# Chunked attention and a Fourier-mixed MLP: later stores of untouched weight blocks, and ten slab loads moved into the next product

## The chip, the cores and the metric

The kernel runs on one core of one Trainium2 chip. The metric is the device time of one execution in microseconds (us); less is better. All arithmetic is in single precision.

## The reference, cut to what matters

```
# B, H, S, D = 8, 8, 576, 64;  chunks of 64 tokens, 9 a sequence
scores = q_c @ k_c^T / sqrt(D)              # inside each chunk
x = softmax(scores) @ v_c                   # -> (B, S, 512)
u = x + real(fft(fft(x, axis=1), axis=2))
un = (u - mean(u)) / sqrt(var(u) + 1e-6)    # along the last axis
out = u + max(un @ w_ch1, 0) @ w_ch2        # w_ch1: 512 x 2048, w_ch2: 2048 x 512, given in double precision
```

## The kernel before, in words

**Groups.** The 4608 tokens are cut into nine groups of 512 (`NG = 9`). Each group passes through `mlp(g)`: a first product with `w_ch1` and a second one with `w_ch2`. Attention and Fourier mixing of batch b (`attention`, `fourier`, joined in `side(b)`) are emitted in slices between the steps of the product of the group before it. The whole instruction order is written out by hand (`manual_schedule`). The main loop counts steps: `t` goes up by one for every `yield` of `mlp`. Group 0 takes steps 1 to 16 for its first product and 17 to 32 for its second (`KF = 16` row blocks each); `begin[1]` is 32. `ready_at[0]` is 2 * 16 - 5 = 27.

**Each engine works its queue in order.** SP issues nearly all loads and stores (908 of the DMAs), so a load stands behind every store that the program names before it; all of them go into one hardware queue, q1, and are served by 16 DMA engines.

**Weights.** The weights come as 32 pieces of 512 KB of doubles. Pieces 0 to 15 make `w1` (the tile `wa`), pieces 16 to 31 make `w2` (the tile `wb`), one a row block: piece 16 + m is row block m of `w2`. `load_weight` (L348) issues a load. `round_weight` turns doubles into floats: a head for piece i (DVE L372, L382; ACT L364, L367, L370) and a tail for piece i - 1 (DVE L379, L380, L388), after which the raw space is free and the next load is issued. `round_next` does the next piece; the counter is `n_w`. The two spaces that hold the last pieces are rows of `xall` that `keep2` (POOL L1095) writes afterwards.

**Block forms of the products.** From group 1 on, both products are done in seven half-size products instead of eight. The weight blocks and their sums that these need are written to DRAM while group 0 runs, `s1` for the first product and `s2` for the second, and are read back as slabs:

- `keep2(i)` makes four sums of `w2` blocks on POOL; `keep2_store` (L1107) stores them to `s2`.
- `keep2_whole(i)`, for i = 0 to 3, stores three blocks that need no sum, straight from `w2`: row blocks 2i, 2i+1 and 8+2i, 8+2i+1. It is three DMAs of 256 KB (L1114).
- `keep1(pair)` makes the sums of `w1` (POOL L1078) in the space of `w2` rows that are done with; `keep1_store` (L1082) stores them to `s1`.

For `keep2_whole` the loop body has, behind the call of `round_next`:

```
while n_whole < HF // 2 and n_w > KF + HF + 2 * n_whole + 2:
    keep2_whole(n_whole)
    n_whole += 1
keep2_store()
```

`KF + HF` is 24, so the four calls come as soon as 26, 28, 30 and 32 pieces have been counted.

**Slabs.** `fetch(1)` (L1179) loads the next of 196 slabs of 256 KB for the first product (28 a group, groups 2 to 8) into a ring of `NS1 = 10` in `wa`. Ten are fetched ahead when group 1 is at its middle, and every turn of `up_halves` (28 a group, the matmuls of L1309) fetches one more into the slot that the turn has read. So the last ten turns of a group fetch the first ten slabs of the next one. `fetch(2)` (L1184) does the like for the second product of groups 1 to 6 (`down_halves`, L1363).

**The last two groups.** Groups 7 and 8 (`FEW = 7`) do their second product in `down_few`: 26 quarter-size products (L1427), listed in `PRODUCTS`. Their slabs, 512 KB each, come by `fetch(3)` (L1182) through a ring of ten, one after each product. Twenty-three of these blocks are sums that `make_rest` makes on POOL and DVE (L1156) from the middle of group 6 to the end of the first product of group 7; it reads its inputs (L1145) and stores the sums (L1163) on SP too.

Of the kernel before, what the change touches and what calls it, by code (L numbers as in the profile page):

```python
# [16 lines left out]
def kernel(  # L17
# [43 lines left out]
    KF = DFF // 128  # L61
# [41 lines left out]
    NO, HF = 7, KF // 2  # L103
# [3 lines left out]
    NS1, NS2, Z1, Z2 = 10, 3, 2 * 2 * 128, HF * HM  # L107
# [958 lines left out]
    def parts1(pair):  # L1066
        a11, a12, a21, a22 = w1_part(pair, 0, 0), w1_part(pair, 0, 2), w1_part(pair, 1, 0), w1_part(pair, 1, 2)
        o1, o2, o4 = (made1(pair, j) for j in range(3))
        return a11, o2, o1, a21, a12, o4, a22
# [46 lines left out]
    def block_of(name):  # L1116

        if name[0] == "s":
            return s3[STORED.index(name)]
        o, k = (2, "dw".index(name)) if name in "dw" else ({"b1": 0, "b2": 0, "b3": 4 + "12".index(name[2]), "b4": 4 + "12".index(name[2])}[name[:2]], (int(name[1]) - 1) % 2)  # L1120
        return s2[o, :, k * Z3:(k + 1) * Z3]
# [49 lines left out]
    FEW = NG - 2  # L1171
    first_of = {1: 1, 2: 1}
    n_slab = {1: 0, 2: 0, 3: 0}

    def fetch(which):
        i = n_slab[which]
        if which == 1 and i < HF // 2 * NO * (NG - 2):
            pair, o = divmod(i % (HF // 2 * NO), NO)
            nc.sync.dma_start(out=slab1[i % NS1].rearrange("p k r f -> p (k r f)"), in_=s1[pair, UP[o]])  # L1179
        elif which == 3 and i < NR2 * (NG - FEW):  # L1180
            to = slab3[i % NS3].rearrange("p m e -> p (m e)")
            nc.sync.dma_start(out=to, in_=block_of(PRODUCTS[i % NR2][1]))  # L1182
        elif which == 2 and i < NO * (FEW - first_of[2]):
            nc.sync.dma_start(out=slab2[i % NS2].rearrange("p m e -> p (m e)"), in_=s2[i % NO])  # L1184
        n_slab[which] = i + 1
# [3 lines left out]
    def operands(h1, m):  # L1189

        nc.vector.tensor_tensor(out=xs[:, m], in0=h1[:, m, hi], in1=h1[:, HF + m, hi], op=ALU.add)  # L1191
        nc.vector.tensor_tensor(out=ys[:, m], in0=xs[:, m], in1=h1[:, m, lo], op=ALU.subtract)
        nc.gpsimd.tensor_tensor(out=h1[:, m, hi], in0=h1[:, m, lo], in1=h1[:, m, hi], op=ALU.subtract)  # L1193
# [94 lines left out]
    def up_halves(g):  # L1288
        unT = unTs[g]
        h1 = one_p.tile([128, KF, G * 128], FP32, tag="big", name="h1")  # L1290
        t1, t2, t4 = tt_1 if g == 1 else (tt[:, o] for o in range(3))
        rhs = (unT[:, 0:2, lo], t2, t1, unT[:, 0:2, hi], unT[:, 2:4, lo], unT[:, 2:4, hi], t4)
        for pair in range(HF // 2):
            pas, pbs = {}, {}
            for turn_, o in enumerate(UP):
                if g == 1:
                    w = parts1(pair)[o].rearrange("p k (r f) -> p k r f", r=2)
                else:
                    w = slab1[((g - 2) * HF // 2 * NO + pair * NO + turn_) % NS1]
                for r in range(2):  # L1300
                    m = 2 * pair + r
                    a, b = (tmp_1 if g == 1 else tmp)[:, r, 0], (tmp_1 if g == 1 else tmp)[:, r, 1]
                    if o == 0:
                        pas[r] = ps_f.tile([128, 2, 256], FP32, tag="ff", name="pa")
                    if o == 1:
                        pbs[r] = ps_f.tile([128, 2, 256], FP32, tag="ff", name="pb")
                    dst = (pas, pbs, pas, pbs, pas, pas, pbs)[o][r][:, (0, 0, 1, 1, 0, 1, 1)[o]]
                    for kk in range(2):
                        nc.tensor.matmul(  # L1309
                            out=dst, lhsT=w[:, kk, r], rhs=rhs[o][:, kk],  # L1310
                            start=(o in (0, 1) and kk == 0), stop=(kk == 1), skip_group_check=True,
                        )
                    if o == 0:
                        nc.scalar.copy(a, dst)  # L1314
                        nc.vector.tensor_tensor(out=b, in0=pbs[r][:, 0], in1=a, op=ALU.add)  # L1315
                    elif o == 2:
                        nc.vector.tensor_tensor(out=a, in0=dst, in1=b, op=ALU.add)  # L1317
                        if g == 1 and pair == 0:
                            combined(1, r, True)
                    elif o == 3:  # L1320
                        nc.vector.tensor_tensor(out=h1[:, HF + m, hi], in0=dst, in1=a, op=ALU.add)
                        if pair > 0 and g < FEW:
                            operands(h1, m - 2)
                    elif o == 4:
                        nc.scalar.activation(out=h1[:, m, lo], in_=dst, func=ACTF.Relu)  # L1325
                    elif o == 5:
                        nc.vector.tensor_tensor(out=h1[:, m, hi], in0=dst, in1=b, op=ALU.add)
                        nc.scalar.activation(out=h1[:, m, hi], in_=h1[:, m, hi], func=ACTF.Relu)
                    elif o == 6:
                        nc.vector.tensor_tensor(out=h1[:, HF + m, lo], in0=dst, in1=b, op=ALU.add)  # L1330
                        nc.scalar.activation(out=h1[:, HF + m], in_=h1[:, HF + m], func=ACTF.Relu)  # L1331
                if g > 1:
                    fetch(1)
                if pair == HF // 4 and turn_ > 0 and g >= FEW:
                    sums(h1, EARLY.split()[turn_ - 1:turn_], nc.vector if g == FEW else nc.gpsimd)
                if turn_ in (1, 3, 5, 6):
                    yield h1
        for m in (HF - 2, HF - 1) if g < FEW else ():
            operands(h1, m)
# [67 lines left out]
    def down_few(g, h1):  # L1407
        banks, begun = {}, set()
        left = [sum(p[3].count(f"{i + 1}{j + 1}") for p in PRODUCTS for j in range(2)) for i in range(G)]
        sums(h1, ["a24=a23+a24"])  # L1410
        for o, (a, _, bank, reads, then) in enumerate(PRODUCTS):
            w, lhs = slab3[((g - FEW) * NR2 + o) % NS3], block_a(h1, a)
            half = int(bank.isupper())
            if bank not in banks:
                if half:
                    banks[bank] = banks[bank.lower()]
                else:
                    banks[bank] = ps_f.tile([128, 2, 256], FP32, tag="ff", name="dn")
                begun.add(bank)
                fresh = True  # L1420
            else:
                fresh = False
            dst, k = banks[bank][:, half], o // 2
            if o % 2 and g + 1 < NG and k in range(5, 5 + 2 * G, 2):
                turned(g + 1, (k - 5) // 2)
            for m in range(4):
                nc.tensor.matmul(  # L1427
                    out=dst, lhsT=lhs[:, m], rhs=w[:, m],
                    start=(fresh and not half and m == 0), stop=(m == 3), skip_group_check=True,
                )  # L1430
            for sign_, i, j in zip(reads[0::3], reads[1::3], reads[2::3]):
                i, j = int(i) - 1, int(j) - 1
                n = groups[g][i]
                to = os_[:, i, j * HM:(j + 1) * HM]
                base = to if (i, j) in begun else natural(n)[:, j * HM:(j + 1) * HM]
                begun.add((i, j))
                nc.vector.tensor_tensor(out=to, in0=base, in1=dst, op=ALU.add if sign_ == "+" else ALU.subtract)
                left[i] -= 1
                if left[i] == 0:
                    store(n, os_[:, i])  # L1440
            sums(h1, then.split())
            fetch(3)
            if o % 2 == 0:
                continue
            if g + 1 < NG:
                for j in range(G):
                    if k == 3 + 2 * j:
                        normed(g + 1, j)
                    if k == 5 + 2 * j and j >= 2:
                        combined(g + 1, j - 2)  # L1450
            yield
# [7 lines left out]
    with tc.manual_schedule():  # L1459
# [22 lines left out]
        n_w = 2  # L1482
# [40 lines left out]
        ready_at = [begin[g] + (2 * KF - 5 if g < first_of[2] else 2 * HF + 4) for g in range(NG)]  # L1523
# [12 lines left out]
        n_whole, n_kept, late, rest_ = 0, 0, [], None  # L1536
        conv2 = chain(conv2)
        t = 0
        for g in range(NG):
            for _ in mlp(g):  # L1540
# [24 lines left out]
                    if t <= 2 or t < KF and t % 4 == 0 or t >= KF + 3:  # L1565
                        round_next()

                while n_whole < HF // 2 and n_w > KF + HF + 2 * n_whole + 2:
                    keep2_whole(n_whole)
                    n_whole += 1  # L1570
                keep2_store()
# [22 lines left out]
                for _ in range(2 if t > begin[1] else 0):  # L1594
                    if put_off:
                        b, t0_, r, o = put_off.pop(0)
# [60 lines left out]
```

## Time and profile before

| | |
|---|---|
| runs | 1063.61, 1063.99, 1064.34 us; median 1063.99 us |
| the profiled execution | 1063.73 us, of which the profile's span is 1061.9 us |
| TensorE (PE) busy | 1043.3 us, 98% of the span |
| VectorE (DVE), GpSimd (POOL), ScalarE (ACT) busy | 626.5, 431.9, 315.5 us |
| DMA | 219.10 MB, 206 GB/s on the mean |
| mean granted TensorE clock | 0.998 |

From the span's start, in us: 0 to 50 the attention and the Fourier mixing of batch 0; about 50 to 116 the first product of group 0; 116 to 191 its second product, with batch 1 beside it and the rounding of `w2`; 191 to 249 the first product of group 1 and so on; from 868.0 to 916.8 the first product of group 7, to 964.3 its second, to 1012.8 the first product of group 8, and its second to the end.

A page of the profile gives for each engine the time in which it worked. Rows by window (a stretch of the span) give the same for that stretch, with the clock that TensorE was granted, the busy share of the 16 DMA engines, and what they moved. A timeline row begins with the start and the time taken, and ends, where the engine was idle before it, with the idle time and what ended it. L numbers are lines of the kernel before. A row of SP is the issue of a DMA, not its run.

### The profile page before, as it was taken

The numbers are of one execution on the slowest core, as the hardware profiler recorded it, in microseconds if no ns is written. First come the engines' busy times: TensorE is split into PE (matmuls) and PEld (weight loads), VectorE is DVE, ScalarE is ACT, GpSimd is POOL, SyncE is SP. The second block draws the span as 40 slices with busy tenths as digits, with TensorE's granted clock in tenths as the row PEclk, the third lists the DMA queues.
The fourth block names the chain that finished last, engine by engine and source line by source line (L and its number), as shares of the span: only waits on it lengthen the run. The fifth ranks groups of instructions, "written<-read, shape, count | busy, mean of one in ns | idle before, by whom it ended". The sixth has DMA issues, their size and how long they took to land.

```text
span 1061.9 us, 20222 instructions
## 1 busy us (share of the span) xinstructions
PE 1043.3 (98%) x7482; PEld 851.6 (80%) x7482; DVE 626.5 (59%) x1339; ACT 315.5 (30%) x744; POOL 431.9 (41%) x555
## 2 busy tenths in 40 slices
PE   7999999999999999999999999999999999999998
PEld 6645444788888888888888888888888888888887
DVE  4798986974567465664565645745664666443332
ACT  4688573233113311332022312331133103201200
POOL 3410119753425151244134421514252777660282
PEclk9999999999999999999999999999999999999999
DMA  8767675687688447973678357944753759998364
GB/s 169 221 197 213 163 218 199 203 233 230 231 215 230 134 142 214 250 207 108 186 229 223 118 169 231 250 131 155 215 168 102 269 187 353 363 399 279 89 216 142
DMA packets 167088, 219.10 MB, mean 206 GB/s; under 512 B 77228, under 2 KB 111020, under 8 KB 161614
## 3 DMA queue, kind: packets, MB, share of 16 engines
q1 hardware_dynamic: 155978, 211.98, 64.8%
q0 software_dynamic: 9024, 4.91, 2.1%
q8 instruction: 60, 0.98, 0.4%
q10 hardware_dynamic: 1988, 0.92, 0.3%
q14 instruction: 38, 0.31, 0.1%
HBM read 183.61 MB, written 34.08 MB: 205 GB/s over the span
## 4 chain that ended last, share of the span: by engine, by line
PE 79%; DVE 6%; DMA 4%; ACT 3%; POOL 3%; SPq 2%; issue 2%; DVEq 0%; ACTq 0%; POOLq 0%
PE pa L1309 20%; PE pb L1309 15%; PE pb L1363 14%; PE pa L1363 11%; PE dn L1427 7%; PE pt L399 2%; SPq L265 2%; PE mix L840 2%; PE xp L501 2%; PE z L722 1%; DMA xall<-in_moe_w_ch_dram 1%; PE up L1219 1%; PE sc L451 1%; POOL h L1207 1%; POOL part L1156 1%
## 5 line engine op out<-in xcount | busy, mean ns | idle before, releaser
L1309 PE MATMUL pa<-unT,wa 128*128 128x256 f32 x736 | 175.3, 381 | 0.2 <-DVE xall L1317 0.2
L1309 PEld LDWEIGHTS pa<-unT,wa 128*128 128x128 f32 x736 | 138.1, 190 | 19.6 <-DVE xall L1317 0.6
L1309 PE MATMUL pb<-wa 128*128 128x256 f32 x448 | 106.6, 381 | 0.0
L1309 PEld LDWEIGHTS pb<-wa 128*128 128x128 f32 x448 | 84.3, 190 | 11.5
L1363 PE MATMUL pa<-wb,h 128*128 128x256 f32 x384 | 87.2, 380 | 0.0
L1363 PE MATMUL pb<-wb,h 128*128 128x256 f32 x384 | 86.4, 379 | 0.0
L1193 POOL TENSOR_TENSOR h<-h 128x256 f32<-128x256 f32 x48 | 40.8, 858 | 98.2 <-DVE wb L1191 91.6
L1363 PEld LDWEIGHTS pa<-wb,h 128*128 128x128 f32 x384 | 71.8, 190 | 9.7
L1363 PEld LDWEIGHTS pb<-wb,h 128*128 128x128 f32 x384 | 72.0, 190 | 9.4
L1044 POOL DMA_DIRECT2D out_dram<-wb x28 | 18.8, 674 | 121.8 <-DVE wb L1380 71.9
L1315 DVE TENSOR_TENSOR wa<-pb,wa 128x256 f32<-128x256 f32 x56 | 23.7, 424 | 63.5 <-ACT wa L1314 63.5
L1309 PE MATMUL pb<-unT,wa 128*128 128x256 f32 x256 | 60.6, 379 | 0.1
L1325 ACT ACTIVATE h<-pa 128x256 f32<-128x256 f32 x64 | 24.6, 384 | 115.0 <-PE pa L1309 114.1
L1260 PE MATMUL dn<-wb,h 128*128 128x512 f32 x128 | 58.7, 608 | 0.0
L1314 ACT COPY wa<-pa 128x256 f32<-128x256 f32 x56 | 20.9, 372 | 121.4 <-PE pa L1309 121.4
L1309 PEld LDWEIGHTS pb<-unT,wa 128*128 128x128 f32 x256 | 48.6, 190 | 7.1 <-DVE wa L1315 0.5
L1207 POOL TENSOR_TENSOR h<-h 128x512 f32<-128x512 f32 x34 | 42.8, 1276 | 27.2 <-ACT h L1331 24.1
L1309 PE MATMUL pa<-wa 128*128 128x256 f32 x224 | 53.9, 383 | 0.0
L483 ACT COPY pT<-pt 128x512 f32<-128x512 f32 x36 | 21.0, 582 | 105.8 <-PE pt L399 105.5
L1331 ACT ACTIVATE h<-h 128x512 f32<-128x512 f32 x64 | 40.0, 630 | 39.5 <-DVE h L1330 39.1
L1219 PE MATMUL up<-unT,wa 128*128 128x512 f32 x108 | 49.4, 598 | 0.0
L857 POOL TENSOR_TENSOR xall<-y,xall 128x513 f32<-128x513 f32 x14 | 22.3, 1590 | 61.1 <-DVE y L851 45.0
(312 smaller groups left out, 2136.6 us busy)
## 6 DMA issues: line engine op xcount, KB each, us to landing
wa<-s SPq DMA_DIRECT2D x196, 256.0 KB
wb<-s SPq DMA_DIRECT2D x42, 1024.0 KB
wb<-s SPq DMA_DIRECT2D x32, 512.0 KB
xall<-in_moe_w_ch_dram SPq DMA_DIRECT2D x22, 512.0 KB
q<-in_q_dram SPq DMA_DIRECT2D x96, 112.0 KB
k<-in_k_dram SPq DMA_DIRECT2D x96, 112.0 KB
s<-part SPq DMA_DIRECT2D x32, 256.0 KB
v<-in_v_dram SPq DMA_DIRECT2D x124, 64.0 KB
```

The costliest lines, as they stand in the source:

```text
L265: eng.dma_start(out=t[p0:p0 + np_], in_=src[b, :, c * CH:c * CH + np_, :].rearrange("h p d -> p h d"))
L857: eng.tensor_tensor(out=x[:, 0:w], in0=y[:, 0:w], in1=x[:, 0:w], op=ALU.add)
L1193: nc.gpsimd.tensor_tensor(out=h1[:, m, hi], in0=h1[:, m, lo], in1=h1[:, m, hi], op=ALU.subtract)
L1207: eng.tensor_tensor(out=out_, in0=a, in1=b, op=op)
L1219: nc.tensor.matmul(out=up, lhsT=w1[:, kk, m * 128:(m + 1) * 128], rhs=unT[:, kk], start=(kk == 0), stop=(kk == KD - 1), skip_group_check=True,
L1260: nc.tensor.matmul(out=dn, lhsT=h1[:, m, s * 128:(s + 1) * 128], rhs=w2[:, m, :], start=(m == 0), stop=(m == KF - 1),)
L1309: nc.tensor.matmul(out=dst, lhsT=w[:, kk, r], rhs=rhs[o][:, kk], start=(o in (0, 1) and kk == 0), stop=(kk == 1), skip_group_check=True,)
L1315: nc.vector.tensor_tensor(out=b, in0=pbs[r][:, 0], in1=a, op=ALU.add)
L1325: nc.scalar.activation(out=h1[:, m, lo], in_=dst, func=ACTF.Relu)
L1331: nc.scalar.activation(out=h1[:, HF + m], in_=h1[:, HF + m], func=ACTF.Relu)
L1363: nc.tensor.matmul(out=dst, lhsT=lhs[:, m], rhs=w[:, m], start=(o in (0, 2) and m == 0), stop=(m == HF - 1), skip_group_check=True,)
L1427: nc.tensor.matmul(out=dst, lhsT=lhs[:, m], rhs=w[:, m], start=(fresh and not half and m == 0), stop=(m == 3), skip_group_check=True,)
```

## The change

Two things are moved; nothing is added or left out.

1. `keep2_whole(0)` to `keep2_whole(3)` are no longer tied to the count of rounded pieces. They come one a step at `t` = 24, 25, 26 and 27 (`t > ready_at[0] - 4`), ahead of that step's `keep2_store`.
2. The first ten slabs of the last group's first product are no longer fetched in the last ten turns of group 7's `up_halves`. When `n_slab[1]` has reached 28 * 6 = 168, group 7 stops fetching; the ten are fetched in group 7's `down_few` after its products 10 to 19, one each, behind that product's `fetch(3)`.

```diff
@@ up_halves @@
-                if g > 1:
+                if g > 1 and (g != FEW or n_slab[1] < HF // 2 * NO * (FEW - 1)):
                     fetch(1)
@@ down_few @@
             sums(h1, then.split())
             fetch(3)
+            if g == FEW and 10 <= o < 10 + NS1:
+                fetch(1)
             if o % 2 == 0:
                 continue
@@ main loop @@
-                while n_whole < HF // 2 and n_w > KF + HF + 2 * n_whole + 2:
+                if n_whole < HF // 2 and t > ready_at[0] - 4:
                     keep2_whole(n_whole)
                     n_whole += 1
                 keep2_store()
```

## The prediction

> **What bounds the kernel now.** I read the page's busy times first, then the windows, to see in which stretches the busiest engine has anything to lose, then what TensorE (PE) waits for, and then the queues that feed that wait.
>
> ```profile
> PE 1043.3 (98%) x7482; PEld 851.6 (80%) x7482; DVE 626.5 (59%) x1339; ACT 315.5 (30%) x744; POOL 431.9 (41%) x555
> ```
>
> PE is idle for 18.6 us of 1061.9. The windows (length, then busy time of PE, PEld, DVE, ACT and POOL, then the granted clock, DMA share and GB/s) say where:
>
> ```profile
> 0.00:50.00 50.00, 42.32 (x516) 31.16 (x516) 29.47 (x87) 26.56 (x67) 21.42 (x48) 1.00 0.79 201
> ...
> 150.00:200.00 50.00, 45.32 (x243) 25.97 (x241) 39.60 (x65) 19.34 (x52) 38.58 (x32) 0.97 0.64 203
> 200.00:300.00 100.00, 99.66 (x856) 85.45 (x857) 61.78 (x136) 26.76 (x69) 48.02 (x67) 1.00 0.70 221
> ...
> 916.00:965.00 49.00, 48.58 (x233) 42.24 (x232) 19.88 (x46) 2.34 (x5) 28.94 (x24) 1.00 1.02 394
> ```
>
> 7.7 us lie in the first 50, which the change does not touch, 4.7 us between 150 and 200, and 4.3 us behind the last products. From 200 to the end of PE's work only fractions are left. PE's waits after 200 (sum, times, longest) are three rows; the only one in the stretches of the second edit is the first:
>
> ```profile
> PE dn L1427 <- POOL h L1207: 0.4, 1, 0.4
> PE pb L1309 <- DVE h L1321: 0.3, 1, 0.3
> PE pa L1309 <- DVE xall L1317: 0.2, 1, 0.2
> ```
>
> So the change can win in two places: about 2.5 of the 4.7 us at 150 to 200, and at most 0.5 us near 930. It can lose wherever it makes PE wait.
>
> The big wait at 150, in PE's timeline, is the mixing matmul behind ACT's copy of zf:
>
> ```profile
> 155.25 0.49 PE L840 MATMUL mix<-ce,zf 128*128 128x129 f32 x2 [2.47 <-ACT zf L773]
> ```
>
> ACT had waited for DVE's zs (L752, L756). The DVE timeline shows why those were late (the bracket is the idle time before a row):
>
> ```profile
> 144.72 0.43 DVE L372 TENSOR_SCALAR power<-xall 128x512 uint32<-128x512 uint32 x1 [0.75 <-DMA xall<-in_moe_w_ch_dram]
> ...
> 146.62 0.67 DVE L388 TENSOR_TENSOR wb<-wb,power 128x512 f32<-128x512 f32 x1
> 149.83 0.43 DVE L372 TENSOR_SCALAR power<-xall 128x512 uint32<-128x512 uint32 x1 [2.54 <-DMA xall<-in_moe_w_ch_dram]
> ...
> 152.32 0.75 DVE L752 TENSOR_TENSOR zs<-more_z,zs 128x580 f32<-128x580 f32 x1
> ```
>
> DVE stood 2.54 us for a weight piece, with the zs operations queued behind it. SP's queue shows what was ahead of that piece:
>
> ```profile
> 134.38 0.35 SPq L348 DMA_DIRECT2D xall<-in_moe_w_ch_dram  x1
> ...
> 136.86 3.53 SPq L348 DMA_DIRECT2D xall<-in_moe_w_ch_dram  x2
> 140.44 1.53 SPq L1114 DMA_DIRECT2D s<-wb  x3
> 142.02 0.63 SPq L1082 DMA_DIRECT2D s<-wa  x1
> 143.06 3.66 SPq L348 DMA_DIRECT2D xall<-in_moe_w_ch_dram  x2
> ```
>
> The three L1114 are `keep2_whole(0)`: 768 KB in front of the load issued at 143.06.
>
> **Edit 1, the stores of whole blocks.** Emission moves from the steps in which the pieces are counted to steps 24 to 27. SP's L1082 at 142.02 belongs to step 20, so the first call leaves its place ahead of the load at 143.06 and lands behind the last load (146.4).
>
> Load, issue to the DVE that it released: 134.38 to 138.40 is 4.02 us; 136.86 to 141.41 is 4.55; the second of that pair, issued about 140.05 (the group's end, 140.39, less one issue of 0.35), to 144.72 is 4.67; the one in question, 143.06 to 149.83, is 6.77. Its issue doesn't move: it waits for DVE's L382 at 142.95. With one 256 KB store ahead of it, as the 4.55 one had, it lands at 147.6; the bounds are 147.1 and 147.7. DVE itself is free at 147.29. So DVE resumes at 147.3 to 147.7 and gains 2.1 to 2.5 us; I take 2.3. A load at 140.05 that is also quicker, with less behind it (4.02 instead of 4.67), would free DVE by up to 0.65 earlier and let the gain reach 2.7.
>
> Does the gain reach the end? Step by step. zs needs ACT's L747, done at 148.84, and would start at 152.32 - 2.3 = 150.0: no wait. The last piece, issued at 146.38, lands by 146.4 + 4.67 = 151.05; DVE wants it at 153.85 - 2.3 = 151.55: no wait, with 0.5 us to spare. PE finishes the matmuls before the gap at 152.78 and the mixing could start at 155.25 - 2.3 = 152.95. Behind it stand the last tails on DVE (159.16), POOL's `keep2` sums, which write the rows that those tails free (POOL L1095 at 155.55 and 159.85 both wait for DVE L380), then POOL L857 at 164.48, statistics, `un`, the transposes, L1031 to L1033, and the first L1309 of group 1 at 191.39. PE, ACT, DVE and POOL each run in order, no link of this chain is tied to a clock of its own, so it moves as a block. PE has no work to be late with: its idle 0.40, 0.53 and 1.14 us at 171 to 182 stay. From 191 on PE is nearly solid and hands the shift on to the end. Minus 2.3 us.
>
> What the moved stores cost where they go: twelve SP issues of about 0.45 us. The first two calls fit into 146.8 to 161.4, where SP had held nine of them anyway. Calls three and four come behind L1107 of step 25, at about 162 to 166, six issues, 2.7 us of SP, 1.5 MB. Behind them on SP are stores, L1107 of yall, gated by POOL until 169.4 anyway, and L1082; no load stands there before L252 at 184.45. Their readers come late: `fetch(2)` first at 229.7, and POOL's reuse of the space (the second keep2 set at 178.36 and 183.39). DMA moved 63 GB/s between 171.2 and 182.4, so the 3.6 us that 1.5 MB takes at 420 GB/s fits. Cost nothing, covered by that lull; without it, up to 3.6 us on the load of L252.
>
> **Edit 2, the ten slabs.** Out of 894 to 926 go ten issues and 2.6 MB. There DMA is full, but PE's only wait is the 0.42 us for POOL sums, which start when the matmuls allow and not when a DMA lands: gain 0, bound 0.4. In: ten issues behind ten `fetch(3)` in products 10 to 19, PE time 936.6 to about 953.
>
> ```profile
> 936.60:951.30 14.70, 14.70 (x74) 12.94 (x73) 6.49 (x13) 0.59 (x1) 8.85 (x7) 1.00 1.02 419
> 951.30:964.30 13.00, 13.00 (x66) 11.51 (x65) 6.03 (x15) 0.59 (x1) 0.78 (x2) 1.00 0.98 336
> ```
>
> A product is eight matmul rows in 1.73 us, so 512 + 256 KB every 1.73 us is 454 GB/s, more than the 419 that moved here. Over ten products the queue falls behind by 10 x (786 KB / 419 GB/s - 1.73) = 1.5 us, and by some 1.2 us for the output stores among them. But a product's slab is asked for ten products, 17 us, ahead, and the 2.6 MB (6.2 us at 419) that have left the stretch before let SP start this one without arrears. The ten slabs themselves are wanted from 964.3 on, one each 1.73 us, some 26 us behind their issue. Cost 0; upper bound 6.2 us, all ten transfers laid bare.
>
> On this edit the Trainium skill ("DMA: Bandwidth & Descriptors", Specifications) speaks against the change: it gives 358 GB/s as one core's share of HBM and 435 as the fabric's ceiling, and neither reaches the 454 that this edit asks for. The trace's 419 lies between the two. By 358 the arrears would be an estimated 4.7 us instead of 1.5, and the sum still the same.
>
> **The clock.** PE's gap cost clock as well:
>
> ```profile
> 152.60:156.00 3.40, 0.93 (x6) 0.74 (x6) 3.37 (x8) 2.00 (x7) 0.45 (x1) 1.00 0.96 261
> 156.00:159.50 3.50, 3.50 (x8) 1.84 (x7) 3.07 (x3) 3.12 (x10) 2.54 (x2) 0.51 0.04 13
> ```
>
> After 2.47 us idle the clock was 0.51 for 3.5 us: some 1.7 us of PE time lost. PE then ran into its wait at 171.21 all the same, so winning them back only lengthens that wait from 0.40 to about 2.1 us. That new gap could throttle 169 to 173, and PE's slack behind it (0.53 + 1.14) just about pays for 1.7 us. If not, about 1.2 us come back.
>
> The skill ("TensorE: Matmul & The Clock Gate", Why this matters for your kernels) says that gaps up to about 3 us keep the clock. The trace's 2.47 us did not; by the page the 1.2 us could never come back, by the row they can.
>
> **Sum.** 1063.73 for the profiled execution (1061.9 of span and 1.8 around it) less 2.3 is 1061.4; the median lies 0.26 above that execution, so 1061.6.
>
> **Rivals.** (a) The gap moves: the wait at 171 throttles the clock and 1.2 us return, 1062.8. For: the same length of gap did it once. Against: there is slack to pay. 0.12. (b) The piece lands late for another reason (its own two neighbours on the queue), or the zs wait passes to the last piece: 1063 to 1064. Against: three loads in 4.0 to 4.7 us. 0.12. (c) Slower: the second product of group 7 starves. The place is products 10 to 25; it decides if slabs land more than 17 us behind their issue. The price is up to 6.2 us, giving 1063 to 1067.8, mostly over 1066. For: DMA share 1.02 there already. Against: arrears of a few us by the sums above. 0.14. (d) Edit 2 does not do what it says: at group 7's start 10 + 5 x 28 = 150 slabs have been fetched, the 168 are reached after 18 turns, and ten are left for ten products. Excluded.
>
> **How the numbers follow.** Forecast 0.62: gain 1.8 to 2.7, with the spread of the runs 1061.0 to 1062.2 on its own. The difference that a measurement can tell is 0.2%, 2.1 us, so faster means below 1061.86: which takes a gain over 2.1 and so 0.45 of the forecast's 0.62. Slower, above 1066.1: most of (c) and something for unknowns, 0.14. Same: the rest, 0.41. For 8 in 10 the range reaches down to 1060.8 (gain 2.7 and the 0.4 of edit 2) and up to 1064.4, which takes in (a) and (b) and leaves most of (c) out.
>
> **What would show it.** Right: L1114 behind the last L348; DVE L372 at 147.3 to 147.7 with hardly a wait; PE's 2.47 us row under 0.5 us and no 0.51 clock at 156; first L1309 at 189.1; L1427 without a DMA row. Wrong: the 2.5 us still ahead of L372, a wait at POOL L1078 or L1095 for a store, or PE L1427 or L1309 behind wb or wa loads after 936.

## The result, and the profile after

| | before | changed |
|---|---|---|
| median of nine runs each, side by side | 1063.99 us (1062.93 to 1065.19) | 1060.12 us (1058.99 to 1062.19) |
| profiled execution, its span | 1063.73, 1061.9 us | 1062.15, 1060.3 us |

The ratio is 0.9967, with a 95% interval of 0.9958 to 0.9976: faster by 3.5 us (2.6 to 4.5). The forecast was 1061.6 with a range from 1060.8, so the gain was underrated by about 1.5 us, and the time lies just below the range. The profiled execution of the changed kernel is one of three late ones among its nine (1062.15 to 1062.19); where this one is late is the first reading below, and the other two have no trace.

The windows of the changed kernel (length, busy time of PE, PEld, DVE, ACT and POOL, granted clock, DMA share, GB/s) show three changes. At 11.6 the clock is half, where it was full before. The hole in front of the mixing is gone (3.27 of 3.40 us busy, before 0.93), and so is the half clock behind it. And from 916 to 935 PE has no hole:

```profile
11.60:18.40 6.80, 6.12 (x70) 4.65 (x72) 1.38 (x2) 2.68 (x5) 0.00 (x0) 0.50 0.91 184
...
152.60:156.00 3.40, 3.27 (x14) 1.86 (x13) 3.40 (x7) 2.68 (x8) 1.15 (x1) 1.00 1.11 343
156.00:159.50 3.50, 3.50 (x11) 1.64 (x10) 3.04 (x4) 2.45 (x9) 2.19 (x3) 1.00 0.45 151
916.00:935.00 19.00, 19.00 (x90) 16.73 (x89) 6.82 (x17) 0.83 (x2) 17.56 (x15) 1.00 1.02 384
```

The first row stands in code that the change doesn't touch, in a start that is 1.64 us longer than that of the kernel before; this hides part of the gain in the spans. How much of it the half clock made is not shown: a trace further below has a start nearly as long (117.61 us) with the clock at 1.00 throughout. To keep such things apart I cut every trace at four marks: PE's first matmul of L1260 (group 0), its first mixing matmul behind that (L840), the first L1309 of group 1, the first L1427 of group 7. The tail is the stretch from there to PE's last end. Lengths in us; a span is the sum of the five and 4.2 behind PE's last end.

| kernel | to L1260 | to the mixing | to L1309 | to L1427 | tail | span |
|---|---|---|---|---|---|---|
| before | 116.47 | 38.78 | 36.14 | 725.38 | 140.89 | 1061.89 |
| changed | 118.11 | 36.44 | 36.16 | 725.39 | 140.05 | 1060.32 |

The span fell by 1.57: the start gave away 1.64, the second part won 2.34 and the tail 0.84. Two parts moved that the change touches, one for each edit.

**Edit 1** as SP and DVE show it. SP's queue in the changed kernel, where the three stores of L1114 now stand behind the last load:

```profile
145.52 2.81 SPq L348 DMA_DIRECT2D xall<-in_moe_w_ch_dram  x2
148.38 1.55 SPq L1114 DMA_DIRECT2D s<-wb  x3
```

And DVE, whose wait for the piece was 2.54 us (the bracket):

```profile
149.13 0.43 DVE L372 TENSOR_SCALAR power<-xall 128x512 uint32<-128x512 uint32 x1 [0.22 <-DMA xall<-in_moe_w_ch_dram]
151.62 0.75 DVE L752 TENSOR_TENSOR zs<-more_z,zs 128x580 f32<-128x580 f32 x1
```

Less the 1.64 of the start, L372 is at 147.49 and L752 at 149.98, for which 150.0 was forecast. PE's wait moved from the mixing to the next `un`, where it is 2.11 us instead of 0.40:

```profile
170.53 0.63 PE L399 MATMUL pt<-ident,un 128*128 128x128 f32 x4 [2.11 <-DVE y L851]
```

**Edit 2** as PE shows it. A product of L1427 takes 1.73 us from start to start. Before, two of them in a row came clearly late: 930.58 to 932.89 is 2.31, and 932.89 to 934.80 is 1.91.

```profile
930.58 1.89 PE L1427 MATMUL dn<-more,h 128*128 128x256 f32 x8
932.89 1.97 PE L1427 MATMUL dn<-more,yall 128*128 128x256 f32 x8 [0.42 <-POOL h L1207]
934.80 1.53 PE L1427 MATMUL dn<-wb,yall 128*128 128x256 f32 x6
```

In the changed kernel they follow each other in 1.73:

```profile
929.90 1.89 PE L1427 MATMUL dn<-more,h 128*128 128x256 f32 x8
931.63 1.89 PE L1427 MATMUL dn<-more,yall 128*128 128x256 f32 x8
933.36 1.89 PE L1427 MATMUL dn<-wb,yall 128*128 128x256 f32 x8
```

The bracket blames POOL. But POOL's sums of L1207 run in one unbroken string in both kernels, and in the changed one PE starts the same product inside a sum: from 929.54 on each takes about 1.3 us, so the first two end at 930.8 and 932.2, and PE starts at 931.63.

```profile
929.54 7.60 POOL L1207 TENSOR_TENSOR h<-h 128x512 f32<-128x512 f32 x6
```

Both kernels have the same compute instructions here, so this product can need at most the first of these sums. In the kernel before, that one ended at 931.5, 1.4 us ahead of PE's start at 932.89; the sum that the bracket means is the second, which ended at 932.87.

What differs is the slab that this product reads. In SP's queue before, loads of `wa` (two of the ten moved) stand between the two loads into `more`, and the second of these is issued at 925.35, 7.5 us ahead of PE's start:

```profile
920.60 1.01 SPq L1179 DMA_DIRECT2D wa<-s  x2
924.03 0.32 SPq L1182 DMA_DIRECT2D more<-s  x1
924.44 0.86 SPq L1179 DMA_DIRECT2D wa<-s  x2
925.35 0.42 SPq L1182 DMA_DIRECT2D more<-s  x1
```

In the changed kernel both are out by 921.3, over 10 us ahead:

```profile
920.50 0.80 SPq L1182 DMA_DIRECT2D more<-s  x2
921.39 5.57 SPq L1182 DMA_DIRECT2D wb<-s  x6
```

So after the result the theory was: PE waited at 932.89 for a slab, not for POOL, and the size of that wait differs from one execution to the next. The rival that the experiments were set against: the wait is POOL's, and the 1.5 us too much are the chance of the runs.

### The profile page after: what moved, and what is told of

Same layout as the page of the kernel before. It is cut to its first block, busy times and chain, and to the rows that moved or that the text cites. A ratio compares the mean times of both kernels' runs of the same rounds, so it can differ in the third digit from the quotient of the medians.

```text
span 1060.3 us, 20226 instructions
## 1 busy us (share of the span) xinstructions
PE 1043.2 (98%) x7482; PEld 852.8 (80%) x7482; DVE 626.4 (59%) x1339; ACT 315.2 (30%) x744; POOL 431.5 (41%) x555
## 4 chain that ended last, share of the span: by engine, by line
PE 86%; DVE 4%; SPq 3%; ACT 3%; DMA 2%; issue 1%; POOL 0%; DVEq 0%; ACTq 0%; POOLq 0%
PE pa L1309 20%; PE pb L1309 15%; PE pb L1363 15%; PE pa L1363 12%; PE dn L1427 8%; PE dn L1260 3%; PE pt L399 3%; PE up L1219 2%; PE z L722 2%; PE xp L501 2%; SPq L265 2%; PE mix L840 2%; DMA xall<-in_moe_w_ch_dram 1%; PE sc L451 1%; PE up_a L1219 0%
## 5 line engine op out<-in xcount | busy, mean ns | idle before, releaser
L1309 PE MATMUL pa<-unT,wa 128*128 128x256 f32 x736 | 175.3, 381 | 0.2 <-DVE xall L1317 0.2
L1309 PEld LDWEIGHTS pa<-unT,wa 128*128 128x128 f32 x736 | 138.1, 190 | 19.6 <-DVE xall L1317 0.6
L1309 PE MATMUL pb<-wa 128*128 128x256 f32 x448 | 106.6, 381 | 0.0
L1309 PEld LDWEIGHTS pb<-wa 128*128 128x128 f32 x448 | 84.3, 190 | 11.5
L1315 DVE TENSOR_TENSOR wa<-pb,wa 128x256 f32<-128x256 f32 x56 | 23.7, 424 | 63.4 <-ACT wa L1314 63.4
L1309 PE MATMUL pb<-unT,wa 128*128 128x256 f32 x256 | 60.6, 379 | 0.1
L1260 PE MATMUL dn<-wb,h 128*128 128x512 f32 x128 | 57.4, 596 | 0.0
L1309 PEld LDWEIGHTS pb<-unT,wa 128*128 128x128 f32 x256 | 48.6, 190 | 7.1 <-DVE wa L1315 0.5
L1207 POOL TENSOR_TENSOR h<-h 128x512 f32<-128x512 f32 x34 | 42.6, 1272 | 27.6 <-ACT h L1331 24.1
L1309 PE MATMUL pa<-wa 128*128 128x256 f32 x224 | 53.9, 383 | 0.0
L857 POOL TENSOR_TENSOR xall<-y,xall 128x513 f32<-128x513 f32 x14 | 22.3, 1590 | 61.1 <-DVE y L851 45.0
```

What stands on the lines that cost most here:

```text
L857: eng.tensor_tensor(out=x[:, 0:w], in0=y[:, 0:w], in1=x[:, 0:w], op=ALU.add)
L1207: eng.tensor_tensor(out=out_, in0=a, in1=b, op=op)
L1260: nc.tensor.matmul(out=dn, lhsT=h1[:, m, s * 128:(s + 1) * 128], rhs=w2[:, m, :], start=(m == 0), stop=(m == KF - 1),)
L1309: nc.tensor.matmul(out=dst, lhsT=w[:, kk, r], rhs=rhs[o][:, kk], start=(o in (0, 1) and kk == 0), stop=(kk == 1), skip_group_check=True,)
```

## The experiments

Each kernel is timed against the kernel before, side by side. Ratios stand with their 95% intervals. There were three comparisons, each on another chip, with their own runs of the kernel before: 1063.46 us (29 runs) beside each edit alone, both again and the first call at its old place; 1063.60 (20 runs) beside POOL's sums, both places, the clock and the two additions; 1063.39 (29 runs) beside half the slabs and the kernels run once more. Differences from the kernel before are within a comparison. Where a kernel is set against the changed one, that is its run in the first comparison (1059.69).

### Edit 1 alone

```diff
-                while n_whole < HF // 2 and n_w > KF + HF + 2 * n_whole + 2:
+                if n_whole < HF // 2 and t > ready_at[0] - 4:
```

> Edit 1 alone: the whole-block stores at steps 24 to 27, the slab loads as before. Theory: the gain of the change is the sum of two independent ones, 2.3 us where DVE no longer stands behind the stores of call 0, and 0.76 us near 930 from edit 2. Then this run gains 2.3 us (1063.99 to about 1061.7), its PE row near 930 still waits some 0.4 us, and no PE row waits 2.47 us at 152 to 155. Rival (all of the gain is edit 1, and the 0.76 is a follow-up of it): 3.1 us and no wait near 930.

1062.54 us, 0.9988 (0.9977 to 0.9999): 0.9 us gained, where 2.3 were expected. The way to the mixing is nevertheless 36.39 us, like the changed kernel's 36.44. The tail is 141.32, and PE's waits after 200 are one row, which now has another name:

```profile
PE dn L1427 <- DMA more<-s: 0.9, 1, 0.9
```

In PE's timeline it is the same product, 2.79 us behind the one ahead of it (927.29):

```profile
930.08 1.97 PE L1427 MATMUL dn<-more,yall 128*128 128x256 f32 x8 [0.90 <-DMA more<-s]
```

Its slab was issued at 922.68, 7.4 us earlier, as in the kernel before (7.5). POOL's sums end here at 929.5 and 930.7 by their durations, neither of them at 930.08. The wait follows the slab.

### Edit 2 alone

```diff
-                if g > 1:
+                if g > 1 and (g != FEW or n_slab[1] < HF // 2 * NO * (FEW - 1)):
...
+            if g == FEW and 10 <= o < 10 + NS1:
+                fetch(1)
```

> Edit 2 alone: the ten slabs in products 10 to 19 of group 7, the stores as before. Theory (PE waited near 930 for late slabs of 512 KB, not for the POOL sums that the profile names): 0.6 to 0.8 us gained, about 1063.2, the 0.42 us row near 932 gone, the 2.47 us row at 152 kept. Rival, the prediction's own step (PE waits there for POOL sums): no gain, 1064.0, and the row stays.

1062.66 us, 0.9994 (0.9984 to 1.0003). The way to the mixing is 38.54, as before, the tail 140.05 without a row for L1427. Edit 2 therefore does take the tail's lateness away on its own, and what that is worth lies within what the runs can tell.

### Both again

The changed kernel, in the same comparison as the three kernels with parts of it:

> The changed kernel once more, on the chip of the three parts. Theory: the sum of its parts, 3.1 us gained (1060.9), in two groups of executions about 2 us apart, the later ones with a granted clock under 1 that comes from the first 20 us of the span. Rival (the parts work on each other): over 0.7 us more or less than the two parts together.

1059.69 us, 0.9965 (0.9953 to 0.9977). The way to the mixing is 36.28, the tail 140.05, the start 115.51. This time none of five executions was late (1059.48 to 1059.93), and the gain is 3.8 us. That is 2.1 more than the two parts together (0.9 and 0.8), which was the rival's sign, that the parts work on each other; the repeats further below make this difference smaller.

### The first call of the whole blocks at its old place

Edit 1 with the first `keep2_whole` where it was, the other three late:

```diff
-                while n_whole < HF // 2 and n_w > KF + HF + 2 * n_whole + 2:
+                if n_whole < HF // 2 and (n_w > KF + HF + 2 if n_whole == 0 else t > ready_at[0] - 3):
```

> Edit 1 without its first call: call 0 stays where it was, ahead of the load at 143, calls 1 to 3 at steps 25 to 27; slab loads as before. Theory (only the 768 KB ahead of the weight load count): no gain, 1063.7 to 1064.2, DVE's wait of 2.5 us before L372 stays. Rival (the other nine stores, behind the last load or later, count as well, through the last piece or SP's freedom): a part of the 2.3 us, over 0.7.

1064.24 us, 1.0006 (0.9998 to 1.0015). PE's gap before the mixing is 2.21 us and the way there 38.53: the first call's 768 KB alone cost what edit 1 gains. The tail is 143.16, 3.1 us over 140.05, with two rows that both name slabs:

```profile
PE dn L1427 <- DMA more<-s: 1.2, 1, 1.2
PE dn L1427 <- DMA xall<-s: 0.8, 1, 0.8
```

### POOL's sums on VectorE

Edit 1, and the sums that stand ahead of the late product on DVE instead of POOL, so that POOL can't be the one that PE waits for:

```diff
-            sums(h1, then.split())
+            sums(h1, then.split(), nc.vector if g == FEW and o == 8 else nc.gpsimd)
```

> Edit 1 alone, with the six sums behind product 8 of group 7 on DVE in place of POOL. Theory (PE waits near 930 for the 512 KB slabs of products 6 to 10): PE still waits there, 0.4 to 3 us in all, from execution to execution, and the time is that of edit 1 alone, about 1062.5. Rival (the prediction's reading of the row: PE waits for POOL's sums): the wait is gone, at most 0.1 us left, and the time falls by 0.5 or more.

1064.43 us, 1.0011 (1.0000 to 1.0023). PE's waits:

```profile
PE dn L1427 <- DVE wb L1437: 2.9, 1, 2.9
PE dn L1427 <- DMA more<-s: 0.3, 1, 0.3
```

The expected 1062.5 was missed, because the edit made a wait of its own: the sums delayed DVE's L1437, and PE stood 2.9 us for that at 938.05. The slab's row comes 9 us ahead of this, at 929.14: the product starts 2.18 us behind the one before it, instead of 1.73. So it is late without the six sums on POOL, which speaks for the slab, if with a small wait. The time of this kernel says nothing on the question.

### The ten slabs loaded in both places

Both edits, and the ten loads issued at their old place too, into the same slots:

```diff
                 if g > 1 and (g != FEW or n_slab[1] < HF // 2 * NO * (FEW - 1)):
                     fetch(1)
+                elif g == FEW:
+                    i = n_slab[1] + pair * NO + turn_ - 18
+                    p_, o_ = divmod(i % (HF // 2 * NO), NO)
+                    nc.sync.dma_start(out=slab1[i % NS1].rearrange("p k r f -> p (k r f)"), in_=s1[p_, UP[o_]])
```

> Both edits, and the ten slabs also loaded at the old place, in the last ten turns of group 7's first product (the later loads bring the same data once more). Theory (these 2.6 MB in the queue at 894 to 926 make the slabs of products 6 to 10 late): PE waits near 930 again, 0.4 to 3 us, and the time goes back to that of edit 1 alone, 1061 to 1063, with more spread. Rival (the later place itself has the merit, by the order of the last loads): the time stays at 1059.7.

1062.01 us, 0.9989 (0.9976 to 1.0001), 2.3 over the changed kernel. The tail is 142.45 and the rows are back (L1427 is L1431 in this kernel):

```profile
PE dn L1431 <- DMA more<-s: 0.6, 1, 0.6
PE dn L1431 <- POOL h L1207: 0.6, 1, 0.6
```

It is the ten loads' traffic in that place that makes the slabs late, and not anything else that edit 2 does. The second row again names POOL, for the product ahead of the late one (928.48); in the changed kernel that product starts at 929.90, inside the first of the sums that the row means, so it doesn't need it.

### Half the slabs

Both edits, with the first five of the ten slabs left at their old place and the last five moved:

```diff
-                if g > 1 and (g != FEW or n_slab[1] < HF // 2 * NO * (FEW - 1)):
+                if g > 1 and (g != FEW or n_slab[1] < HF // 2 * NO * (FEW - 1) + 5):
...
-            if g == FEW and 10 <= o < 10 + NS1:
+            if g == FEW and 15 <= o < 10 + NS1:
```

> Both edits, but only five of the ten slabs are moved, to products 15 to 19; the other five stay in the first product of group 7. Theory (bytes ahead of the slabs of products 6 to 10 make them late): between the changed kernel (1059.7) and edit 1 alone (1062.5), 1060 to 1061.5, and group 7's second product to PE's end 140.05 to 141.5. Rival (only the last few loads or only the first few matter): equal to one of the two ends.

1059.84 us, 0.9971 (0.9960 to 0.9983); tail 140.05. As good as the whole edit, so the theory's even share for each load missed. The run points to the last five as those that cost: they stand among the 512 KB loads in SP's queue (five L1179 from 920.60 to 926.2 in the kernel before). With seven executions and one trace this is a hint, since a trace of the kernel before, with all ten in place, has the same tail (below).

### Keeping the clock up

Both edits and three dummy matmuls in the attention of batch 0, against the half clock at 11.6:

```diff
+        if n == 1:
+            keep_warm(1)
...
+        keep_warm(1)
...
+            if n == lo:
+                keep_warm(1)
```

> Both edits, and three more idle matmuls of 128x289 in PE's idle times at about 8.4, 10.4 and 12.2 us. Theory (the later group of executions, 1062.2, is those in which the clock was halved at 11.6 to 18.4 because PE was little used before): no execution over 1061, no row of 0.5 clock before 100, and the median at 1059.5 to 1060.0. Rival (the start's spread is that of the first loads): the two groups stay, or every execution is 0.3 us or more longer.

1060.08 us, 0.9968 (0.9955 to 0.9982), a little over the expected range. Its trace has no half clock before 100, and none of its five executions is late, but neither was one of the five of the same kernel without the dummies, whose median is 0.4 lower. Inconclusive: with three late executions in nine and none in five, five runs can't tell.

### Two additions on VectorE

After edit 1 PE waits 2.1 us for `un`, whose `y` comes through POOL's L857. Both edits, with the batch-1 additions on DVE:

```diff
-            eng = nc.gpsimd if kind(n) == HI else nc.vector
+            eng = nc.gpsimd if kind(n) == HI and b > 1 else nc.vector
```

> Both edits, and the two additions of batch 1's reversed tiles (POOL L857 at 163.8 and 170.5 in the changed kernel) on DVE, which idles 2.67 us for the first of them. Theory (what is left between 165 and 182 is the chain POOL sums, L857, statistics, un, y): the first addition ends at about 162.2 instead of 165.0, PE's 2.1 us row at 168 falls under 0.4, and 1.7 to 2.0 us are gained on both edits, about 1057.9. Rival (PE or ACT is next at once): under 0.7 us.

1057.63 us, 0.9945 (0.9930 to 0.9960), 2.1 under the changed kernel and the fastest of all (four executions). From the mixing to L1309 it takes 34.91 us instead of 36.14, and 0.7 more come in the stretch to L1427, for which no row gives the reason. The moved gap is therefore a real loss that can be worked on; it didn't fall under 0.4 as expected but is now split into two, 0.66 and 1.79 us (PE's waits between 150 and 200):

```profile
PE pt L399 <- DVE y L851: 2.5, 2, 1.8
```

### The kernel before, and each edit alone, once more

The gains of the parts (0.9 and 0.8) do not add up to that of both (3.8), so all three were run again.

> The kernel before, for a second trace of it. Theory (its spread of 4 us is the start, 115 to 118 us to the first L1260, and the wait for late slabs of group 7's second product): from the first L1309 of group 1 to group 7's second product 725.4 us again, from there to PE's end between 140.4 and 143.5, where the kernels with edit 2 have 140.05; a part of it in rows behind more or xall slabs. Rival (the first trace's 0.84 is the rule): 140.7 to 141.0.

The kernel before, against itself: 1064.57 us, 1.0011 (1.0001 to 1.0020). The same code thus reads 1.2 us slower, at an interval that just excludes no difference. Two series of runs of one program differed by that much here, so a difference of 1 us between two kernels means little.

Its trace has no slab row and a tail of 140.05, where more lateness was expected. The time went elsewhere: to L1427 it takes 728.90 us instead of 725.38. DVE's timeline in that run:

```profile
873.95 0.69 DVE L1156 TENSOR_TENSOR part<-part,xall 128x512 f32<-128x512 f32 x1 [5.61 <-DMA s<-part]
```

and in the first run of the same kernel:

```profile
869.94 3.17 DVE L1156 TENSOR_TENSOR part<-part,xall 128x512 f32<-128x512 f32 x1 [1.27 <-DMA s<-part]
```

By the chain of what released what, the store of 256 KB behind this ran from 865.53 for 4.31 us in the first trace and from 865.24 for 8.61 us in the second, and so released DVE 4 us later, with L1315 queued behind; PE lost 1.97 us in its wait and most of the rest to a half clock behind it (eight matmuls in 3.37 us instead of 1.89). After this delay the slabs were in time, which is not what was expected.

It fits the theory all the same. Between the issue of the second slab in `more` and the start of the product that reads it lie 7.1 to 7.7 us in the six traces in which this product is late, and 8.0 us or more in the eight in which it isn't: 7.54 and late in the first trace of the kernel before, 8.17 and in time in the second, 8.02 in the kernel with half the slabs, 10.77 in the changed one.

> Edit 1 alone once more. Theory (edit 1 is worth 2.2 to 2.4 us in its own stretch, whatever the slabs do): first L1260 to the first mixing matmul 36.2 to 36.5 us, and the median 1.5 to 2.5 us under the kernel before of this call. Rival (edit 1 makes the late slabs later): the median under 1.3 us below the kernel before, and 142 us or more for group 7's second product to PE's end.

The kernel with edit 1 alone: 1061.15 us, 0.9977 (0.9967 to 0.9988), 2.2 gained as expected; way to the mixing 36.15, tail 142.17, the same row (the slab in `more`) at 1.2 us. The median is in the theory's range and the tail in the rival's.

> Edit 2 alone once more. Theory: 140.05 us from group 7's second product to PE's end, no row behind slabs, 38.5 us from the first L1260 to the first mixing matmul, and a gain over the kernel before of this call by what its slabs are late, 0.8 to 2 us. Rival (edit 2 pays only with edit 1): under 0.5 us.

The one with edit 2 alone: 1062.56 us, 0.9995 (0.9986 to 1.0004), 0.8 gained, with an interval that includes no gain; way to the mixing 38.33, tail 140.05.

All traces by the same cuts:

| kernel | to L1260 | to the mixing | to L1309 | to L1427 | tail |
|---|---|---|---|---|---|
| before; again | 116.47; 116.23 | 38.78; 38.70 | 36.14; 36.16 | 725.38; 728.90 | 140.89; 140.05 |
| edit 1; again | 115.54; 115.75 | 36.39; 36.15 | 36.13; 36.00 | 725.41; 725.40 | 141.32; 142.17 |
| edit 2; again | 117.61; 115.80 | 38.54; 38.33 | 36.16; 36.13 | 725.39; 725.41 | 140.05; 140.05 |
| both; again | 118.11; 115.51 | 36.44; 36.28 | 36.16; 36.15 | 725.39; 725.51 | 140.05; 140.05 |
| first call early | 115.51 | 38.53 | 36.16 | 725.41 | 143.16 |
| sums on DVE | 115.38 | 36.24 | 36.14 | 725.39 | 143.90 |
| both places | 115.75 | 36.43 | 36.14 | 725.40 | 142.45 |
| half the slabs | 115.57 | 36.75 | 36.14 | 725.42 | 140.05 |
| dummy matmuls | 116.27 | 36.24 | 36.14 | 725.40 | 140.05 |
| additions on DVE | 115.56 | 36.15 | 34.91 | 724.70 | 140.05 |

With the runs of all comparisons put together the medians are 1063.46 for the kernel before (87 runs, without its second series), 1061.52 for edit 1 (23), 1062.62 for edit 2 (23) and 1059.85 for both (14): gains of 1.94, 0.84 and 3.61.

## Why the prediction was wrong

**Edit 1's 2.3 us: right.** DVE resumed 2.34 us earlier less the start, and the way to the mixing is as much shorter (36.15 to 36.75 in the nine traces with all of edit 1, 38.33 to 38.78 in the five without; the means are 2.2 apart). DVE's wait fell from 2.54 to 0.22, and the first L1309 came at 190.71, or 189.07 less the start, where 189.1 was forecast. The block moved as a whole. The cause was right too, as the first call alone brings the loss back. Inside the term there was some luck: in the changed kernel's profile the issue of the load did move, by 0.8 (145.52, or 143.88 less the start, against 143.06), and the load took 3.61 us to its reader instead of the 4.55 assumed; the two cancel. In the first trace of edit 1 alone it took 4.35. Edit 1 alone measured less, 0.9 and 2.2 us under the kernel before. In its traces the tails, 0.4 and 1.3 us longer than the 140.89 of before, took part of it back. They don't tell why the first of the two gains is so small, since that trace is of an execution 1.75 us faster than its median.

**The moved stores and the last piece: right.** No wait for a store appeared at L1078, L1095 or L252, and the way from the mixing to L1309 stayed at 36.16 (36.14 before).

**The clock: right in kind, and worth nothing.** The gap moved to L399 with 2.11 us, for which about 2.1 was forecast. It halved the clock in some traces, as in the one of edit 1 alone:

```profile
168.70:172.20 3.50, 3.50 (x6) 1.33 (x5) 2.26 (x6) 0.82 (x4) 3.42 (x4) 0.51 0.98 360
```

and in others, such as the changed kernel's own, it did not. Both reach L1309 36.13 to 36.16 us behind the mixing, so PE's slack there paid for it: what rival (a) feared happened in these traces without its price. The Trainium skill ("TensorE: Matmul & The Clock Gate", Why this matters for your kernels) says that gaps up to about 3 us keep the clock; this trace's gap of 2.09 us had 0.51 behind it, and the changed kernel's of 2.11 us had 1.00. A gap of 2.87 us kept 1.00 in the kernel with the sums on DVE, and one of 1.97 us had 0.57 behind it in the second trace of the kernel before, so length alone does not decide here.

**Edit 2's cost of 0: right.** No wait for `wb` or `wa` after 936, tail 140.05; rival (c) did not come.

**Edit 2's "gain 0, bound 0.4": this is the step that failed.** It rested on the row that named POOL, and on the sentence that those sums "start when the matmuls allow and not when a DMA lands". The working beside it also took every slab to be asked for 17 us ahead, which leaves no room for a late one; the trace before shows 7.5 us for this slab. The wait was for a 512 KB slab that stood in SP's queue among five of the ten moved loads; POOL's sum merely ended when the slab came. Three readings show this: the row names the slab in both traces of edit 1 alone, PE starts inside the POOL sum that was named once the loads are gone, and the loads put back bring the wait back. The size was wrong as well. Even in the trace before, the loss was the 0.84 us of the tail, twice the bracket, since the next product was late too (1.91 instead of 1.73) and a bracket counts only idle time over a modelled end. In other traces with the loads in place it was 1.27, 2.12 and 3.11 us, and in the second one of the kernel before none. The full DMA share in that stretch (1.02 in the window shown) beside a PE that waited at all was the sign that I passed over.

(The prediction's own sum, 1063.73 - 2.3 + 0.26, is 1061.7 and not 1061.6.) With the term put right, the gain is 2.34 + 0.84 = 3.2 us, which makes 1063.99 - 3.2 = 1060.8 of the median; the measured 1060.12 is another 0.7 lower, which no row of the traces explains. The interval of the gain (2.6 to 4.5 us) holds the 3.2, so the 0.7 need no cause of their own.

That edit 2 is worth more beside edit 1 (1061.52 - 1059.85 = 1.67 us) than without it (0.84) agrees with the tails, 1.27 and 2.12 against 0.84 and 0. A reason lies near: with edit 1 PE comes to the slabs earlier. It is only argued, though. The kernel with the first call early has the largest loss, 3.11, and comes to L1427 at 915.6, between the others; and with such differences between two series of one kernel, 0.8 us is not shown. Whether the two edits help each other stays open.

## What to carry to other kernels

The releaser that a profile names for a short wait is the last event by the profile, not a proven cause: before an edit's gain is set to nothing on that account, check when the data that the instruction reads was issued, and compare starts of successive instructions with their undisturbed distance. Where a queue is served in order at full DMA load, a load that isn't needed yet can delay those that are. A wait of 0.4 us in one trace stood here for a loss of 0 to 3.1 us in others, so bound it by the queue's traffic and not by the row. And a first wait on a chain that is removed shows the next one at the same place: here 2.1 us came up at L399, of which moving two additions won another 2 us.

## What the runs showed of the hardware

- Behind the first L1260, the fourteen traces have seventeen waits of PE of 1.97 to 2.87 us. Eleven were followed by some 3.4 us at about half the clock (0.51 at 156 before and at 168.7 with edit 1 alone), and six by none (2.11 us in the changed kernel; the longest, 2.87 us, in the kernel with the sums on DVE).
- The half clock of 6.8 us at 11.6 in the changed kernel's profile stands in code that no edit touches. The first L1260 came at 115.4 to 118.1 us over the fourteen traces; one of the late ones, at 117.61 with edit 2 alone, has the clock at 1.00 up to there.
- Two series of the same code, side by side, read 1064.57 and 1063.39 us (before; ratio 1.0011, interval 1.0001 to 1.0020). Edit 1 alone read 1062.54 and 1061.15 in two comparisons, with intervals that overlap.
- A 512 KB slab with 256 KB loads between it and the slabs around it reached its reader 7.1 to 7.7 us behind its issue, at a DMA share of 1.01 to 1.04 from 920 to 932 (the six traces in which PE waited for it).
- The wait for one 256 KB store of L1163 held DVE until 869.94 in one trace of the kernel before and until 873.95 in another, though its run began at nearly the same time (865.53 and 865.24).
